# A fused linear attention and two gated feed-forward layers on one core: the attention of the first four half-batches as one chain ahead of everything, with multiplications of a zero tile on TensorE

## The chip, the cores and the metric

The kernel runs on one core of one Trainium2 chip. A core has five engines with instruction queues of their own: TensorE (PE in the profile; its weight loads are shown apart as PEld), VectorE (DVE), ScalarE (ACT), GpSimd (POOL) and SyncE (SP). Each engine takes its instructions strictly in the order in which the program lists them, and waits on semaphores for what other engines or transfers must deliver first. Transfers between the chip's main memory and the on-chip memory are issued from the queues of SP, ACT and POOL and moved by 16 DMA engines. The metric is the device time of one execution in microseconds (us), lower is better; the profile adds one recorded execution.

## The reference

Eight batches with eight heads of 576 positions and 64 channels go through linear attention with a norm; the result, 4608 tokens of 512 channels, goes through two feed-forward layers, all in float32.

```python
kv  = einsum('bhsd,bhse->bhde', k, v)            # 64 x 64 for each head
out = einsum('bhsd,bhde->bhse', q, kv)
rms = sqrt(mean(out * out, axis=-1) + 1e-6)
x   = (out / rms * g_norm)                       # -> 4608 tokens x 512
h   = x @ w_in;  x = (h * cos(h)) @ w_out        # 512 -> 2048 -> 512
a, b = x @ w1, x @ w2                            # 512 -> 1024
out = ((a * b) @ w3) @ w_out2                    # 1024 -> 1024 -> 512
```

## The kernel before, in words

**Numbers.** TensorE multiplies tiles of a type that it takes in one pass and that holds fewer bits than float32. So each float32 operand is split into a high part (a rounding copy, on ACT) and a low part (source minus high part, on DVE or POOL), and a product is three multiplications: high by high, high by low, low by high (`split`, `three`). The kv products of the attention and the sums of squares take float32 tiles as they are.

**Units.** A unit is half a batch, 288 positions; units 0 and 1 are batch 0, units 2 and 3 batch 1, and so on to 15. Heads are taken in pairs (p = 0 to 3), two heads side by side on 128 partitions. For a pair of a batch `emit_kv` makes the two 64 x 64 products of k and v, `evac_kv` splits them into the tile `kv_sb[p]`; for a unit and a pair the queries are split (tile `qhl`), multiplied by kv (`out`), squared (`sq`, ACT) and copied with the norm's weight (`o`, ACT). Sums of squares come from a product with a small selection matrix `sel`. The inverse root is made by three rounds of Newton on DVE (`newton`, 11 small dependent instructions), and `o` is multiplied by it.

**Two ways for the inverse root.** `first_units` handles units 0 and 1: sums land in one PSUM tile `ms_first`, Newton runs on 96 partitions, and TensorE spreads the result over the partitions of `o` by multiplying it with an identity (`spread`). The other units go through `unit_stage`, stage by stage: sums (`ms`), out to main memory (`msd`), back in another shape (`rsx`), Newton, out again (`rsd`) and back as a broadcast (`bc`), four transfers in a row, before `emit_x` multiplies `o`.

**The first feed-forward layer.** Tokens are taken in 9 tiles of 512. A tile's tokens x are split by `split_x` into the tile `x_hl` (one buffer, 4 blocks c of 128 channels). A step n is one block m of 128 of the 2048 hidden channels: `emit_h` (12 multiplications of 128 x 512, into one of two PSUM buffers), the cosine gate on ACT and DVE (`g_first`, `g_rest`; the last DVE instructions of a step are u times h and the low part of g) and, two steps later, `emit_w` (12 more). The order of steps is tile 0 with m = 0 to 7, tile 1 with all 16, tile 0 with 8 to 15, then tiles 2 to 8. Tile 1 needs units 1, 2 and 3.

**Weights.** They arrive as 64-bit numbers and are turned into float32 on chip: a chunk of 128 x 512 takes one ACT instruction (`Abs`) and four on DVE (lines 143 to 150, names `i_f` and `u_f`), then `put` splits it into `w_in` or `w_out` (one ACT copy, one DVE subtraction). 32 chunks belong to the first layer. Eight are converted between `first_units` and the loop over steps, the rest by a rule in the loop.

**The order.** The program is written as above and a list scheduler orders each engine's instructions; an instruction that is written later can stand earlier if its inputs are expected earlier. Units 2 and 3 are written behind the first steps by a table, `quick`, which puts their stages behind steps 0 to 6; their loads go through POOL's queue (`queue(u)`) behind a small GpSimd instruction (`gate`). After the first layer the second one follows, with its weights combined on chip; the change doesn't touch it.

Of the kernel before, what the change touches and what calls it, by code (L numbers as in the profile page):

```python
# [7 lines left out]
F32 = mybir.dt.float32  # L8
# [26 lines left out]
def kernel(  # L35
# [240 lines left out]
    def evac_kv(b, p):  # L276

        ps = kv_ps.pop((b, p))
        for h in range(2):
            d = slice(D * h, D * (h + 1))  # L280
            split(kv_sb[p][d, :, d], ps[d, 0:D], nc.vector)

    def queue(u):

        return nc.gpsimd if 2 <= u < 4 else nc.sync

    def small(u):
        return None if u < 4 else nc.gpsimd
# [62 lines left out]
    def newton(x, y, t):  # L351
# [4 lines left out]
        for _ in range(3):  # L356
            nc.vector.tensor_tensor(t, x, y, ALU.mult)
            nc.vector.scalar_tensor_tensor(t, t, 0.5, y, ALU.mult, ALU.mult)
            nc.vector.scalar_tensor_tensor(y, t, 1.5, y, ALU.subtract, ALU.mult)
# [24 lines left out]
    def emit_x(u, p):  # L384
        o = o_sb[u][:, p, :]
        engine = nc.vector if u < 2 else even(HALF)
# [6 lines left out]
    def first_units(spread):  # L393

        for p in range(NPAIR):
            emit_kv(0, p)
            evac_kv(0, p)
            for u in range(2):
                if p == 0:
                    o_sb[u] = ap.tile([P, NPAIR, HALF], F32, tag="osb", bufs=3, name=f"o_{u}")  # L400
                hl = ap.tile([P, 2, HALF], F32R, tag="hl", bufs=2, name=f"qhl_{u}_{p}")
                split(hl, q_raw.pop((u, p)), nc.vector)
                ps = ps_acc.tile([P, 512], F32, tag=f"acc{(2 * p + u) % 4}", name=f"out_{u}_{p}")
                o, w = ps[:, 0:HALF], kv_sb[p]
# [3 lines left out]
                sq = ap.tile([P, HALF], F32, tag="tmp", bufs=5, name=f"sq_{u}_{p}")  # L408
                nc.scalar.activation(sq, o, AF.Square)
                nc.scalar.activation(o_sb[u][:, p, :], o, AF.Identity, scale=gneg)  # L410
                if p == NPAIR - 2 and u == 1:

                    gate = ap.tile([P, 1], F32, name="gate")
                    marks.append(
                        nc.gpsimd.tensor_tensor(gate, sq[:, 0:1], sq[:, 0:1], ALU.subtract)
                    )

                if p == 0 and u == 0:
                    mst = ps_h.tile([P, 512], F32, tag="h", name="ms_first")
                for k in range(NT3):  # L420
                    at = ((u * NT3 + k) * NPAIR + p) * 2
                    nc.tensor.matmul(
                        mst[0:T3, at:at + 2], sq[:, T3 * k:T3 * k + T3], sel[:, 0:2],
                        start=p == 0 and u == 0 and k == 0, stop=True, skip_group_check=True,
                    )
        n = 4 * NPAIR * NT3
        x, y, t = (row(f"rs_first_{i}")[0:T3, 0:n] for i in range(3))
        nc.vector.tensor_scalar(x, mst[0:T3, 0:n], EPS, HUGE, ALU.add, ALU.min)
        newton(x, y, t)
        for u in range(2):  # L430
            for p in range(NPAIR):
                ps = ps_acc.tile([P, 512], F32, tag=f"acc{p}", name=f"spread_{u}_{p}")
                for k in range(NT3):
                    at = ((u * NT3 + k) * NPAIR + p) * 2
                    for h in range(2):
                        nc.tensor.matmul(
                            ps[D * h:D * h + D, T3 * k:T3 * k + T3],
                            y[:, at + h:at + h + 1].to_broadcast([T3, D]), spread[0:T3],
# [715 lines left out]
```

## Time and profile before

| | us |
|---|---|
| median of 3 runs | 1528.47 (1526.98 to 1534.14) |
| the profiled execution, its own time | 1531.2 |
| its span, first to last instruction | 1529.4 |
| TensorE busy | 1490.5 (97% of the span) |
| VectorE busy | 929.7 (61%) |
| ScalarE busy | 697.0 (46%) |
| GpSimd busy | 370.4 (24%) |

The profiled execution's own time is 1.8 us over its span and 2.7 us over the median. Busy time is the sum of an engine's instructions; a matmul's end is modelled, so a busy TensorE isn't TensorE at its peak rate. Its clock has two levels here, 1.2 and 2.4 GHz; the column PEclk of the windows is the granted share of the higher.

### The profile page before, as it was taken

What the parts mean: (1) busy time and instruction counts of PE and PEld (TensorE: products, weight loads), DVE (VectorE), ACT (ScalarE), POOL (GpSimd) and SP (SyncE); (2) the same over time, 40 slices, a digit from 0 to 9 for tenths busy, and PEclk for the clock granted to TensorE, in tenths of its full rate; (3) what the DMA queues carried; (4) which work ended last, traced back from release to release, by engine and by line L of the source; (5) the groups of instructions that cost most, each with busy time, mean ns of one, the idle gap of its engine ahead of it and who ended that gap; (6) DMA issues with size and microseconds to landing.
All of it is one profiled execution on the core that took longest, in us unless ns stands there. A gap on an engine that the chain in (4) does not pass through costs nothing.

```text
span 1529.4 us, 20532 instructions
## 1 busy us (share of the span) xinstructions
PE 1490.5 (97%) x7616; PEld 1272.5 (83%) x7616; DVE 929.7 (61%) x1714; ACT 697.0 (46%) x1405; POOL 370.4 (24%) x301
## 2 busy tenths in 40 slices
PE   6799999999999999999999998999999999999998
PEld 6577888888887787888888887999999988999997
DVE  3899844576576576666766546755545546545543
ACT  4667654444454454444534335433433334333331
POOL 1111010110010121101102006455444237344330
PEclk9799999999999999999999999999999999999999
DMA  8655120433323424244222005121102313233312
GB/s 292 220 153 167 43 72 5 153 106 114 116 93 102 140 91 146 90 126 123 84 83 79 34 20 215 42 76 67 69 38 83 111 57 113 73 103 124 124 63 76
DMA packets 81956, 156.26 MB, mean 102 GB/s; under 512 B 11600, under 2 KB 37376, under 8 KB 81856
## 3 DMA queue, kind: packets, MB, share of 16 engines
q1 hardware_dynamic: 80240, 150.18, 30.5%
q0 software_dynamic: 1616, 4.78, 1.1%
q8 instruction: 59, 0.97, 0.3%
q14 instruction: 41, 0.34, 0.1%
HBM read 113.77 MB, written 41.15 MB: 101 GB/s over the span
## 4 chain that ended last, share of the span: by engine, by line
PE 86%; DVE 3%; DMA 3%; issue 1%; POOL 1%; ACT 1%; SPq 0%; DVEq 0%; ACTq 0%; POOLq 0%
PE X L767 13%; PE h L533 8%; PE x L535 8%; PE h L534 8%; PE h L535 8%; PE x L533 8%; PE x L534 8%; PE V L767 6%; PE o L534 4%; PE o L533 4%; PE o L535 4%; PE Y L767 3%; PE kv L273 1%; DMA bc<-rsd 1%; PE ms L333 1%
## 5 line engine op out<-in xcount | busy, mean ns | idle before, releaser
L767 PE MATMUL X<-xc,w 128*128 128x384 f32 x1152 | 224.8, 336 | 4.5 <-DVE wchl L115 2.3
L535 PE MATMUL x<-g,w_out 128*128 128x512 f32 x576 | 225.3, 391 | 0.0
L534 PE MATMUL x<-g,w_out 128*128 128x512 f32 x576 | 225.0, 391 | 0.0
L533 PE MATMUL h<-x,w_in 128*128 128x512 f32 x544 | 216.7, 399 | 3.4 <-DVE u L559 2.0
L534 PE MATMUL h<-x,w_in 128*128 128x512 f32 x544 | 214.4, 394 | 1.8 <-DVE x L115 1.8
L533 PE MATMUL x<-g,w_out 128*128 128x512 f32 x576 | 212.6, 391 | 1.5 <-ACT g L113 1.1
L535 PE MATMUL h<-x,w_in 128*128 128x512 f32 x544 | 213.9, 393 | 0.0
L767 PEld LDWEIGHTS X<-xc,w 128*128 128x128 f32 x1152 | 202.9, 188 | 12.1 <-ACT s L775 3.2
L115 POOL TENSOR_TENSOR xc<-x2r,xc 128x768 fp32r<-128x768 f32 x70 | 134.4, 1929 | 229.1 <-ACT xc L113 229.1
L547 ACT ACTIVATE u<-h 128x512 f32<-128x512 f32 x144 | 86.0, 598 | 151.3 <-PE h L535 147.9
L558 ACT ACTIVATE u<-u 128x512 f32<-128x512 f32 x144 | 91.0, 632 | 121.8 <-DVE u L554 107.4
L115 DVE TENSOR_TENSOR g<-u,g 128x512 fp32r<-128x512 f32 x144 | 105.2, 731 | 64.0 <-ACT g L113 63.8
L113 ACT ACTIVATE g<-u 128x512 fp32r<-128x512 f32 x144 | 91.0, 632 | 108.5 <-DVE u L559 85.4
L115 POOL TENSOR_TENSOR qhl<-q,qhl 128x288 fp32r<-128x288 f32 x48 | 42.7, 892 | 395.5 <-ACT qhl L113 316.1
L775 ACT ACTIVATE s<-X 128x384 f32<-128x384 f32 x144 | 66.6, 488 | 152.4 <-PE X L767 152.2
L533 PEld LDWEIGHTS h<-x,w_in 128*128 128x128 f32 x544 | 103.4, 190 | 29.7 <-DVE u L559 5.8
L533 PEld LDWEIGHTS x<-g,w_out 128*128 128x128 f32 x576 | 107.7, 188 | 24.3 <-ACT g L113 1.2
L534 PEld LDWEIGHTS x<-g,w_out 128*128 128x128 f32 x576 | 108.6, 189 | 22.9 <-issue 0.5
L535 PEld LDWEIGHTS x<-g,w_out 128*128 128x128 f32 x576 | 108.4, 188 | 22.8
L559 DVE TENSOR_TENSOR u<-u,h 128x512 f32<-128x512 f32 x144 | 98.5, 684 | 47.2 <-ACT u L558 46.8
L553 DVE TENSOR_SCALAR r<-u 128x512 f32<-128x512 f32 x112 | 49.8, 445 | 123.8 <-ACT u L547 123.7
L534 PEld LDWEIGHTS h<-x,w_in 128*128 128x128 f32 x544 | 103.4, 190 | 23.5 <-DVE x L115 2.5
(183 smaller groups left out, 2653.8 us busy)
## 6 DMA issues: line engine op xcount, KB each, us to landing
x2r<-x_all SPq DMA_DIRECT2D x44, 384.0 KB
kvraw<-in_kv_main_dram SPq DMA_DIRECT2D x28, 512.0 KB
x_all<-x2s SPq DMA_DIRECT2D x36, 256.0 KB
part<-o SPq DMA_DIRECT2D x36, 256.0 KB
part<-part SPq DMA_DIRECT2D x36, 256.0 KB
out_dram<-part SPq DMA_DIRECT2D x36, 256.0 KB
i_w<-in_w1pair_dram SPq DMA_DIRECT2D x16, 512.0 KB
u_w<-in_w1pair_dram SPq DMA_DIRECT2D x16, 512.0 KB
```

The lines of the kernel that those rows point to most:

```text
L113: hi = nc.scalar.activation(dst[:, 0], src, AF.Copy)
L115: lo = lo_engine.tensor_tensor(dst[:, 1], src, f32(dst[:, 0]), ALU.subtract)
L273: nc.tensor.matmul(ps[d, 0:D], k[:, d], v[:, d], start=i == 0, stop=i == NC)
L533: nc.tensor.matmul(ps, w[0], x[0], start=first, stop=False)
L534: nc.tensor.matmul(ps, w[0], x[1], start=False, stop=False)
L535: nc.tensor.matmul(ps, w[1], x[0], start=False, stop=last)
L547: nc.scalar.activation(u, h_ps[n], AF.Identity, bias=0.25, scale=INV_2PI)
L553: nc.vector.tensor_scalar(r, u, ROUND, ROUND, ALU.add, ALU.subtract)
L558: nc.scalar.activation(u, u, AF.Sin, scale=-TWO_PI_DOWN)
L559: nc.vector.tensor_tensor(u, u, h_ps.pop(n), ALU.mult)
L767: nc.tensor.matmul(ps, w[:, self.i, a, k], x[:, b, k], start=first and k == 0 and n == 0, stop=last and k == 1 and n == 2, skip_group_chec ...
L775: copied.append(nc.scalar.activation(s, ps, AF.Copy).ins)
```

## The change

What it does:

- All four units of batches 0 and 1 go through `first_units`, as one chain of eight steps (b, p), written in the order in which the engines are to take it; inside `manual_schedule` the scheduler leaves DVE, ACT and PE in that order. A step is: products with the queries (`outs`), squares, then kv, queries and kv's split of the next pair, then sums of squares of this one, four multiplications of a zero tile (`idle_work`: 256 columns, result never read), the weighted copies, and, behind pairs 1 and 3 to 7, a weight chunk converted (`convert(1)`) and an earlier one split (`put(1)`).
- 28 multiplications of the zero tile stand ahead of the first kv product.
- The queries' high part is a copy on DVE instead of ACT; kv's split does both high parts, then both low parts.
- Newton runs once, on 96 x 96 numbers for four units instead of 96 x 48 for two; units 2 and 3 get their inverse root through `spread` too. The four transfers in a row, the table `quick` and `gate` are gone for them.
- Loads: queries come for both units of a batch at once, pairs 0 and 1 on ACT's queue; batch 0 and the first weight chunks on SP's; batch 1 and the norm's weight on POOL's. A buffer of batch 0 is used again by batch 1.
- Behind the chain six more chunks are converted instead of eight; `issue_after` orders them and the spreads of units 2 and 3 behind Newton and behind the spreads of units 0 and 1. In the loop, stages of units up to step 31 are ordered behind step n - 2, and their loads behind a weight load.

The diff, cut to its core:

```diff
     def evac_kv(b, p):
         ps = kv_ps.pop((b, p))
-        for h in range(2):
-            d = slice(D * h, D * (h + 1))
-            split(kv_sb[p][d, :, d], ps[d, 0:D], nc.vector)
+        halves = [slice(D * h, D * (h + 1)) for h in range(2)]
+        for d in halves:
+            nc.scalar.activation(kv_sb[p][d, 0, d], ps[d, 0:D], AF.Copy)
+        for d in halves:
+            nc.vector.tensor_tensor(
+                kv_sb[p][d, 1, d], ps[d, 0:D], f32(kv_sb[p][d, 0, d]), ALU.subtract
+            )
     def queue(u):
-        return nc.gpsimd if 2 <= u < 4 else nc.sync
+        return nc.sync
...
+    def load_first():
...
+        qs(0, 0, nc.scalar)
+        qs(0, 1, nc.scalar)
+        kv(0, 0, nc.sync)
+        rest(0, nc.sync)
+        kv(0, 1, nc.sync)
+        prefetch(1)
+        for p in (2, 3):
+            kv(0, p, nc.sync)
+            qs(0, p, nc.sync)
+        rest(1, nc.gpsimd)
         for p in range(NPAIR):
-            emit_kv(0, p)
-            evac_kv(0, p)
-            for u in range(2):
...
+            kv(1, p, nc.gpsimd)
+            qs(1, p, nc.gpsimd)
+        prefetch(8)
...
+        def queries(b, p):
+            for u in range(NHALF):
+                hl = hls[:, (2 * p + u) % 4]
+                q = q_raw.pop((NHALF * b + u, p))
+                nc.vector.tensor_copy(hl[:, 0], q)
+                nc.vector.tensor_tensor(hl[:, 1], q, f32(hl[:, 0]), ALU.subtract)
...
+        for i, (b, p) in enumerate(order):
+            outs(b, p)
+            square(b, p)
+            if i + 1 < len(order):
+                emit_kv(*order[i + 1])
+                queries(*order[i + 1])
+                evac_kv(*order[i + 1])
+            sums(b, p)
+            for _ in range(4):
+                idle_work()
+            keep(b, p)
+            if i in CONVERT:
+                convert(1)
+                if i > CONVERT[0]:
+                    put(1)
+        put(1)
+        nc.vector.tensor_scalar(x, mst[0:T3, 0:NR], EPS, HUGE, ALU.add, ALU.min)
+        last = newton(x, y, t)
...
+    CONVERT = (1, 3, 4, 5, 6, 7)
...
-        first_units(spread)
-        for c in range(KD):
-            split_x(0, c)
-        for _ in range(4):
+        with tc.manual_schedule(
+            engines={
+                mybir.EngineType.DVE, mybir.EngineType.Activation, mybir.EngineType.PE
+            }
+        ):
+            nc.vector.tensor_scalar(gneg, gneg, -1.0, None, ALU.mult)
+            warm = ps_h.tile([P, 512], F32, tag="h", name="warm")
+
+            def idle_work():
+                nc.tensor.matmul(
+                    warm[:, 0:2 * P], kv_warm[:, 0],
+                    kv_warm, start=True, stop=True,
+                )
+
+            for _ in range(28):
+                idle_work()
...
+        for k in range(3):
             prefetch(state["conv"] + 8)
             convert(2)
             put(2)
+        for p in range(NPAIR):
+            rows_of(1, p)
...
-            for u, s in quick.get(n, ()):
-                one = [unit_stage(u, s)]
-                for i in range(4):
-                    run(one, i)
```

How it moves instructions, at two places. First TensorE at the start, around the products of pair 0 with the queries (`out_0_0` is unit 0, pair 0; `kv_0_1` batch 0, pair 1; `warm` the zero tile's result). Before, all four kv products of the batch stand ahead of these rows:

```order
L405 MATMUL out_0_0_159<-qhl_0_0_156,kv0_82 128x288
L406 MATMUL out_0_0_159<-qhl_0_0_156,kv0_82 128x288
L405 MATMUL out_1_0_174<-qhl_1_0_171,kv0_82 128x288
L406 MATMUL out_1_0_174<-qhl_1_0_171,kv0_82 128x288
L407 MATMUL out_0_0_159<-qhl_0_0_156,kv0_82 128x288
L407 MATMUL out_1_0_174<-qhl_1_0_171,kv0_82 128x288
L422 MATMUL ms_first_166<-sel_86,sq_0_0_163 96x2 x3
L405 MATMUL out_0_1_202<-qhl_0_1_199,kv1_83 128x288
```

Now the same engine from the last of the six products of pair 0 on:

```order
L470 MATMUL out_1_0_224<-qhl_first_199,kv0_82 128x288
L273 MATMUL kv_0_1_234<-kvraw_0_1_123 64x64 x8
L273 MATMUL kv_0_1_234<-kvrest_0_121 64x64 x2
L489 MATMUL ms_first_200<-sel_86,sq_0_0_229 96x2 x3
L489 MATMUL ms_first_200<-sel_86,sq_1_0_232 96x2 x3
L1010 MATMUL warm_170<-zeros_97 128x256 x4
L468 MATMUL out_0_1_265<-qhl_first_199,kv1_83 128x288
```

The kv product of the next pair, all sums and four zero products now stand between the products of one pair and of the next, eight times in place of four.

Second VectorE around Newton. Before, Newton (`rs_first`) is mixed with the conversion of the first chunks (`i0_f`, `i1_f`) and with units 2 and 3 (`qhl_2_0` is unit 2, pair 0):

```order
L147 SCALAR_TENSOR_TENSOR i0_f_420<-i0_w_404,i0_f_420 128x512
L144 TENSOR_SCALAR i1_f_423<-i1_f_423 128x512
L359 SCALAR_TENSOR_TENSOR rs_first_1_310<-rs_first_2_311,rs_first_1_310 96x48
L115 TENSOR_TENSOR kv0_82<-kv_1_0_552,kv0_82 64x64
L115 TENSOR_TENSOR qhl_2_1_593<-q_2_1_550,qhl_2_1_593 128x288
L150 SCALAR_TENSOR_TENSOR i0_f_420<-i0_w_404,i0_f_420 128x512
L147 SCALAR_TENSOR_TENSOR i1_f_423<-i1_w_406,i1_f_423 128x512
L357 TENSOR_TENSOR rs_first_2_311<-rs_first_0_309,rs_first_1_310 96x48
```

Now, from Newton's last instruction to the first multiplication of o by the inverse root (`o_0`):

```order
L363 SCALAR_TENSOR_TENSOR rs_first_108<-rs_first_108 96x96
L143 TENSOR_SCALAR i4_f_708<-i4_f_708 128x512
L143 TENSOR_SCALAR u2_f_711<-u2_f_711 128x512
L143 TENSOR_SCALAR i5_f_730<-i5_f_730 128x512
L143 TENSOR_SCALAR u3_f_733<-u3_f_733 128x512
L143 TENSOR_SCALAR i6_f_752<-i6_f_752 128x512
L144 TENSOR_SCALAR i4_f_708<-i4_f_708 128x512
L144 TENSOR_SCALAR u2_f_711<-u2_f_711 128x512
L144 TENSOR_SCALAR i5_f_730<-i5_f_730 128x512
L144 TENSOR_SCALAR u3_f_733<-u3_f_733 128x512
L533 TENSOR_TENSOR o_0_228<-o_0_228,spread_0_0_614 128x288
```

Newton now stands alone behind the whole chain, and five chunks (i4, u2, i5, u3, i6) are converted between it and the last piece of tile 0's split. Counted over the whole list, VectorE has up to that last piece 33 instructions of 128 x 512 with two inputs, 23 with one, 30 of 128 x 288 with two inputs and 4 of 128 x 224, 16 copies of 128 x 288, 16 of 64 x 64 and 11 of Newton.

## Rows read from the trace of the kernel before

**Rows 1.** The page: engines (part 1) and the chain that ended last (part 4).

```profile
PE 1490.5 (97%) x7616; PEld 1272.5 (83%) x7616; DVE 929.7 (61%) x1714; ACT 697.0 (46%) x1405; POOL 370.4 (24%) x301
PE 86%; DVE 3%; DMA 3%; issue 1%; POOL 1%; ACT 1%; SPq 0%; DVEq 0%; ACTq 0%; POOLq 0%
```

**Rows 2.** Windows: stretch, length, busy us of PE, PEld, DVE, ACT, POOL; PEclk, DMA share, GB/s.

```profile
10.00:20.00 10.00, 9.65 (x72) 8.73 (x68) 3.75 (x13) 6.17 (x19) 0.00 (x0) 1.00 0.92 276
...
0.00:58.80 58.80, 41.65 (x355) 34.57 (x356) 35.49 (x98) 31.73 (x80) 8.64 (x26) 0.91 0.83 283
...
58.80:71.30 12.50, 8.13 (x36) 4.95 (x35) 8.61 (x18) 9.01 (x22) 3.07 (x5) 0.91 0.55 178
71.30:112.00 40.70, 40.69 (x209) 31.61 (x209) 37.24 (x89) 26.79 (x55) 7.91 (x11) 0.94 0.50 145
112.00:120.50 8.50, 5.47 (x36) 4.01 (x33) 8.50 (x23) 7.05 (x20) 1.81 (x1) 0.80 0.65 178
120.50:160.00 39.50, 38.84 (x182) 29.96 (x181) 36.16 (x82) 28.87 (x60) 5.73 (x6) 1.00 0.45 140
```

**Rows 3.** Timeline of DVE: start, duration, line, operation, idle before and releaser.

```profile
11.20 0.15 DVE L893 TENSOR_SCALAR gneg<-gneg 128x1 f32<-128x1 f32 x1 [0.55 <-DMA gneg<-in_g_norm_dram]
...
28.07 0.20 DVE L358 SCALAR_TENSOR_TENSOR rs_first<-rs_first,rs_first 96x48 f32<-96x48 f32 x1
28.31 0.20 DVE L359 SCALAR_TENSOR_TENSOR rs_first<-rs_first,rs_first 96x48 f32<-96x48 f32 x1
...
57.46 0.42 DVE L144 TENSOR_SCALAR i_f<-i_f 128x512 int32<-128x512 int32 x1
57.80 0.68 DVE L147 SCALAR_TENSOR_TENSOR u_f<-u_w,u_f 128x512 int32<-128x512 int32 x1
58.40 0.38 DVE L115 TENSOR_TENSOR x<-o,x 128x224 fp32r<-128x224 f32 x1
...
59.30 0.45 DVE L115 TENSOR_TENSOR qhl<-q,qhl 128x288 fp32r<-128x288 f32 x1
59.67 0.68 DVE L150 SCALAR_TENSOR_TENSOR u_f<-u_w,u_f 128x512 int32<-128x512 int32 x1
...
67.07 0.42 DVE L143 TENSOR_SCALAR u_f<-u_f 128x512 f32<-128x512 f32 x1
67.53 0.43 DVE L144 TENSOR_SCALAR u_f<-u_f 128x512 int32<-128x512 int32 x1
```

**Rows 4.** Timeline of PE, three stretches.

```profile
9.52 1.12 PE L273 MATMUL kv<-kvraw 128*64 128x64 f32 x16
...
10.99 1.12 PE L273 MATMUL kv<-kvraw 128*64 128x64 f32 x16
...
13.09 0.44 PE L405 MATMUL out<-qhl,kv 128*128 128x288 f32 x1
13.33 0.44 PE L406 MATMUL out<-qhl,kv 128*128 128x288 f32 x1
...
71.31 0.80 PE L533 MATMUL h<-x,w_in 128*128 128x512 f32 x1 [1.30 <-DVE u L559]
...
126.83 0.29 PE L315 MATMUL out<-qhl,kv 128*128 128x288 f32 x1
126.96 0.29 PE L316 MATMUL out<-qhl,kv 128*128 128x288 f32 x1
```

**Rows 5.** Timeline of ACT: the squares of unit 0, pairs 0 and 3.

```profile
14.05 0.41 ACT L409 ACTIVATE sq<-out 128x288 f32<-128x288 f32 x1 [0.44 <-PE out L407]
...
24.80 0.41 ACT L409 ACTIVATE sq<-out 128x288 f32<-128x288 f32 x1 [1.41 <-PE out L407]
```

**Rows 6.** The chain that ended last, in order of time: start, us, what.

```profile
109.90 3.69 DMA bc<-rsd
```

**Rows 7.** Windows of 2 us later in the first layer, columns as in rows 2.

```profile
504.00:506.00 2.00, 1.49 (x24) 1.38 (x25) 0.58 (x2) 0.22 (x1) 1.77 (x2) 1.00 0.12 48
506.00:508.00 2.00, 2.00 (x7) 1.54 (x6) 0.23 (x1) 1.35 (x4) 0.69 (x1) 0.52 0.58 152
```

More of the change, by code (lines that the diff above doesn't have):

```diff
@@ L428, in first_units @@
[L428 to L438, printed above, removed]
-                            start=k == 0, stop=True, skip_group_check=True,
-                        )
-                o = o_sb[u][:, p, :]
-                nc.vector.tensor_tensor(o, o, ps[:, 0:HALF], ALU.mult)
+                o_ps[NHALF * b + u, p] = o
@@ new lines, in first_units @@
+        order = [(b, p) for b in range(2) for p in range(NPAIR)]
+        emit_kv(*order[0])
+        queries(*order[0])
+        evac_kv(*order[0])
+        for i, (b, p) in enumerate(order):
[13 more added lines that the diff above has]
+                    put(1)
@@ new lines, in rows_of @@
+        def rows_of(b, p):
+            for u in range(NHALF * b, NHALF * b + NHALF):
+                if b == 0:
+                    ps = ps_acc.tile(
+                        [P, 512], F32, tag=f"acc{(2 * p + u) % 4}", name=f"spread_{u}_{p}"
+                    )
+                else:
+                    ps = ps_a.tile([P, 512], F32, tag="pa", name=f"spread_{u}_{p}")
+                mm = scaled(u, p, ps)
+            return mm
+        for p in range(NPAIR + 1):
+            if p < NPAIR:
+                mm = rows_of(0, p)
+            if p > 0:
+                split_x(0, p - 1)
@@ L878 @@
         )
+        for h in range(2):
+            nc.gpsimd.dma_start(
+                out=gneg[D * h:D * h + D], in_=g_norm.rearrange("(d o) -> d o", o=1)
+            )
         def run(stages, i):
@@ L932 @@
             if n < NS:
-                stages = [unit_stage(u, n - w) for u, w in windows.items() if 0 <= n - w <= LAST]
+                with tc.issue_after(word_loads[min(n + 9, n_first - 6)].ins):
+                    stages = [
+                        unit_stage(u, n - w) for u, w in windows.items() if 0 <= n - w <= LAST
+                    ]
                 if more > 0:
@@ L938 @@
                 uu = g_first(n)
-            run(stages, 0)
-            run(stages, 1)
+            gate = ExitStack()
+            if n < 2 * NM:
+                for ins in since[:3 * (n - 1)][-3:]:
+                    gate.enter_context(tc.issue_after(ins))
+            with gate:
+                run(stages, 0)
+                run(stages, 1)
             if n >= 2 and not swap:
                 emit_w(n - 2)
-            run(stages, 2)
+            with ExitStack() as gate:
+                if n < 2 * NM:
+                    for ins in since[:3 * (n - 1)][-3:]:
+                        gate.enter_context(tc.issue_after(ins))
+                run(stages, 2)
             if n < NS:
@@ L954 @@
                         split_x(after, c)
-            run(stages, 3)
-            for u, s in quick.get(n, ()):
-                one = [unit_stage(u, s)]
-                for i in range(4):
-                    run(one, i)
+            with ExitStack() as gate:
+                if n < 2 * NM:
+                    for ins in since[:3 * (n - 1)][-3:]:
+                        gate.enter_context(tc.issue_after(ins))
+                run(stages, 3)
+            if n == 2:
+                behind.close()
             if n == NM + 4:
```

157 lines of the change are left out of this document (103 added, 54 removed), and 3 rows, old and new, of the table quick.

## The prediction

> **What bounds the kernel now.** I read the page first: TensorE is busy 97% of the span and makes 86% of the chain that ended last [rows 1]. So time can only come from stretches in which TensorE waits or runs at its lower clock. The windows show where these lie [rows 2]: in the first 71.3 us TensorE is busy for 41.65 + 8.13 us, and once more from 112 to 120.5, where it is busy 5.47 of 8.5 us. From 120.5 to 160 it lacks 0.66 us. Three moments of the timelines mark the beginning. **A**, 58.8 us: VectorE ends the last piece of tile 0's split (the row at 58.40 lasts 0.38) [rows 3]. **B**, 71.3 us: the third step's first multiplication, let go by VectorE's product u times h [rows 4]. From B on TensorE is busy 40.69 of 40.7 us until the stall at 112 [rows 2]. That stall follows the last transfer of the broadcast for tile 1, which lands at 109.90 + 3.69 = 113.6 [rows 6]; VectorE then has the split of tile 1 to do, in a stretch where it is busy all 8.50 us.
>
> What sets A? VectorE has been busy 35.49 of 58.8 us by then [rows 2], so it waited for 23.3. The change must be judged by VectorE's work up to A, its waits up to A, and the way from A to B; behind B the kernel is TensorE's.
>
> The clock: the granted share reads 1.00 from 10 to 20 us [rows 2], but products of 288 columns stand 0.24 us apart at 13 us and 0.13 apart at 127 us [rows 4], so the chain of before ran at 1.2 GHz, the lower level, and I go by the spacing.
>
> **The change, part by part.** *VectorE's work up to A.* Paces are starts that follow each other [rows 3]: 0.34 us for one input of 512 (57.46 to 57.80), 0.60 for two (57.80 to 58.40), 0.37 for two of 288 (59.30 to 59.67). With the counts given with the change: 33 x 0.60 = 19.8; 23 x 0.34 = 7.8; 34 x 0.37 = 12.6, the four of 224 taken as 288. The copy of 288 with one input isn't in the trace: between 0.19 (0.34 by columns) and 0.37; I take 0.25 since it has one input, 16 x 0.25 = 4.0. The 64 x 64 ones lie between 0 and 0.37, at 0.2 make 3.2. Newton on 96 numbers in a row lies between 0.24 (28.07 to 28.31, 48 numbers) and twice that; fixed cost weighs more at this size, 11 x 0.3 = 3.3. Sum 50.7 us, against 35.5 before: the queries' high parts, units 2 and 3 and four more chunks have moved ahead of A.
>
> *Its waits up to A.* (1) VectorE's first real instruction waits for the norm's weight, which landed at 11.2 us behind four kv loads [rows 3]; it is now behind one small load on another queue. The first pair's loads, 1.3 MB, at 276 GB/s [rows 2] take 5 us and some 2 to start: 7 us. (2) Pairs 0 to 3 need 3.5 MB, and with batch 1's first loads and a weight chunk, which share the engines, about 5.5 MB: at 276 GB/s 20 us, so the split of pair 3's kv ends at about 23.4 us, when VectorE has done some 8 us of work. Issuing from three queues doesn't add to this rate. The Trainium skill says so too (DMA: Bandwidth & Descriptors, "Issuing engines are not separate DMA queues"); no run here separates the queues. (3) Pairs 4 to 7 are paced by an engine. VectorE: conversions now stand alone and depend on each other, which costs 0.46 in place of 0.34, 0.12 more for each (67.07 to 67.53 [rows 3]): a chunk 2 x 0.46 + 2 x 0.72 = 2.4, its split 0.6, queries 1.5, kv 0.4: 4.9 us a pair. TensorE at the lower clock: the pair of before took (24.80 - 14.05) / 3 = 3.58 [rows 5], a kv product 10.99 - 9.52 = 1.47, four zero products of 256 columns 4 x 0.213 = 0.85: 5.9 us a pair. At the higher clock it is near half of that and hidden under VectorE. (4) Behind the last pair: two chunks and three splits, 6.6, and Newton, 3.3.
>
> Newton's end: with the clock up, 23.4 + 3.0 (pair 4 has no chunk) + 3 x 4.9 + 9.9 = 51.0. With the clock down, the first products at 10.3, the eighth pair at 10.3 + 7 x 5.9 = 51.6, + 9.9 = 61.5.
>
> *From Newton to A and B.* 15 x 0.60 + 11 x 0.34 + 18 x 0.37 = 19.4 us, mostly chunk conversions that stand ahead of x. Then 6 us to B: twelve more VectorE instructions stand between the last split and the product that lets step 2 go (6 x 0.60 + 0.34 + 5 x 0.37 = 5.8). Before, this way took 12.5 us, as ACT and VectorE had units 2 and 3 to serve [rows 2]; half of it is saved. B comes at 76.4 with the clock up, 86.9 with it down; before, 71.3. Both ways TensorE has been mostly idle ahead of B, so step 2 starts at the lower clock as before.
>
> *Behind B.* Tile 1's units are ready long before step 8, so the broadcast is gone from the path. The stall was worth 3.03 us of idle time and 0.20 x 8.5 = 1.7 of clock [rows 2]. One buffer holds x, so tile 1's split still waits for step 7; the products of two steps cover it but for perhaps 1 us. I take 4 us back. Loads, stages and order of later tiles differ little: nothing.
>
> *The zero products ahead* take at most 28 x 0.213 = 6.0 us from about 1 us on: they end as the first data lands, and are hidden under it. If the data came at 4.5 us, they would cost 2.
>
> *Sum:* 76.4 - 71.3 - 4 = +1.1 us with the clock up throughout, +11.6 with it down throughout. I take a chain that starts at the higher clock and loses it for part of the pairs, B at 79.5: +4 us. The profiled execution lies 2.7 us above the median; on the median, 1528.5 + 4 = **1532 us**, 0.3% more. A measurement of this kernel can't tell less than 0.5%, 7.6 us, from no change, so I forecast: no change that can be measured.
>
> **The rivals.** *The clock stays down in the chain (slower).* Place: pairs 1 to 7. Price: 5.9 us a pair on TensorE in place of 4.9 on VectorE, B at 86.9, +11.6, so 1540. It decides as soon as TensorE needs over 4.9 us a pair. For it: the kernel of before kept TensorE busy for 9.65 of 10 us between 10 and 20 us with such products and sums of two columns, and it stayed at 1.2 GHz; and after one gap in the stretch 504 to 506, beside a kv product and three with queries, the granted clock was 0.52 [rows 7]. Against it: 28 dense products ahead and four between pairs, which that chain lacked. The Trainium skill speaks against the change here (TensorE: Matmul & The Clock Gate, "A second HAM failure mode: psum-queue depth-cycling"): micro-idles between groups of matmuls make the clock fall and rise again and again. The windows at 504 agree with it, and it would give this rival's 1540.
>
> *Loads come early enough that VectorE never waits after the first data (faster).* Then A comes at 7 + 50.7 + 3 (dependent instructions) = 60.7, B at 66.7, and 71.3 - 66.7 + 4 = 8.6 us are won: 1520. For it: VectorE had 23.3 us of waits to lose and its work is placed into them. Against it: 276 GB/s in the stretch where the loads were the same in kind [rows 2], and VectorE's fixed order, in which pair 3's queries stand ahead of the next conversion.
>
> *The stall at the tile's change stays.* Its 4 us aren't won: 1536 with the rest as forecast. Against it: the broadcast that it followed is gone.
>
> **How the numbers follow.** Forecast 0.45, its own range 1527 to 1537. Clock down 0.25 (1540). No waits 0.17 (1520). Stall stays, or other late waits, 0.13. Slower by over 0.5% (beyond 1536): the clock's 0.25 and most of the last, 0.33. Faster (under 1521): 0.17 and a little for prices that I set too high, 0.20. Within: 0.47. The range takes in the bounds on both sides, 1519 to 1541.
>
> **What would show it.** VectorE's busy time up to the last piece of tile 0's split near 51 us; that moment between 70 and 80 us; B 6 us behind it; conversions 2.4 us each in the chain; kv split of pair 3 at 23 us; no transfer `bc` ahead of step 8 and TensorE idle under 1 us there. The spacing of the products in pairs 4 to 7 tells the clock. I'd be wrong if pairs 0 to 3 come in under 20 us, if VectorE's copies and splits overlap better than their order lets me think, or if stalls behind 160 us, which I leave as they are, change.

## The result, and the profile after

The changed kernel's median is 1538.41 us (8 runs, 1536.36 to 1542.0); the kernel before, run beside it, has 1530.74. The ratio is 1.0051, 95% interval 1.0037 to 1.0066: 7.7 us slower, just over the 7.6 that I called no change, with an interval that reaches to both sides of that bound. The profiled execution took 1542.0, the slowest of the eight and 3.6 us above their median; its span is 1540.2, 10.8 us above the span before. What follows reads this execution.

Its page gives the span and each engine's busy time, and the slices of TensorE's granted clock:

```profile
span 1540.2 us, 20866 instructions
PE 1506.9 (98%) x7804; PEld 1291.6 (84%) x7804; DVE 936.5 (61%) x1709; ACT 693.2 (45%) x1387; POOL 362.0 (24%) x286
PEclk7599999999999999999999999999999999999999
```

TensorE is now idle for 1540.2 - 1506.9 = 33.3 us where it was 38.9, so the change did take idle time away, 5.6 us. But the groups of lines show 13.8 us of zero products:

```profile
L1010 PE MATMUL warm<-zeros 128*128 128x256 f32 x60 | 13.8, 390 | 1.2 <-DVE gneg L976 1.2
```

What is left, 1506.9 - 13.8 = 1493.1, is TensorE's own work, at whatever clock it got: 2.6 more than before's 1490.5. So 13.8 + 2.6 - 5.6 = 10.8. I split every kernel below in these three: idle, zero products, own work. Own work has the same 7744 products in all the changed kernels, so its differences among them come mostly from the clock (ends of products are modelled, so a microsecond more or less says little). The kernel before has 7616: there units 2 and 3 get their inverse root by transfers and not by TensorE.

The windows by stage, to set beside [rows 2], with the same columns: A is now 80.7, B 87.2.

```profile
0.00:58.80 58.80, 47.10 (x364) 42.37 (x364) 32.32 (x82) 27.29 (x67) 8.67 (x24) 0.69 0.66 240
58.80:80.70 21.90, 17.50 (x151) 14.81 (x152) 21.55 (x56) 7.15 (x15) 0.00 (x0) 0.58 0.49 153
80.70:87.20 6.50, 4.81 (x67) 3.32 (x65) 6.04 (x13) 3.95 (x7) 0.00 (x0) 1.00 0.77 251
112.00:128.00 16.00, 15.88 (x71) 12.83 (x70) 15.78 (x38) 11.36 (x28) 0.00 (x0) 1.00 0.04 16
```

The last row is the tile's change: no stall is left there (15.88 of 16 us), and no instruction on `bc` stands ahead of it.

VectorE's timeline at the beginning and at A and B (start, duration, then the instruction, and in brackets what ended the idle time ahead of it):

```profile
10.77 0.15 DVE L1006 TENSOR_SCALAR gneg<-gneg 128x1 f32<-128x1 f32 x1 [9.61 <-DMA gneg<-in_g_norm_dram]
10.84 0.30 DVE L458 CAST qhl_first<-q 128x288 fp32r<-128x288 f32 x1
...
28.30 0.46 DVE L283 TENSOR_TENSOR kv<-kv,kv 64x64 fp32r<-64x64 f32 x2 [0.60 <-ACT kv L281]
...
61.39 0.26 DVE L363 SCALAR_TENSOR_TENSOR rs_first<-rs_first 96x96 f32<-96x96 f32 x1
...
79.94 0.75 DVE L115 TENSOR_TENSOR x<-o,x 128x288 fp32r<-128x288 f32 x2
...
86.51 0.68 DVE L667 TENSOR_TENSOR u<-u,h 128x512 f32<-128x512 f32 x1
```

The multiplication of the norm's weight still heads VectorE's queue and waits until 10.77; all splits of queries stand behind it. TensorE's timeline shows what that does:

```profile
6.72 0.69 PE L273 MATMUL kv<-kvraw 128*64 128x64 f32 x16
11.29 0.37 PE L468 MATMUL out<-qhl_first,kv 128*128 128x288 f32 x1 [3.62 <-DVE qhl_first L458]
12.79 0.61 PE L469 MATMUL out<-qhl_first,kv 128*128 128x288 f32 x1 [1.13 <-DVE kv L283]
13.19 0.45 PE L470 MATMUL out<-qhl_first,kv 128*128 128x288 f32 x1
13.43 0.45 PE L468 MATMUL out<-qhl_first,kv 128*128 128x288 f32 x1
18.69 0.44 PE L468 MATMUL out<-qhl_first,kv 128*128 128x288 f32 x1
30.64 0.44 PE L468 MATMUL out<-qhl_first,kv 128*128 128x288 f32 x1
35.03 0.29 PE L468 MATMUL out<-qhl_first,kv 128*128 128x288 f32 x1
35.16 0.30 PE L469 MATMUL out<-qhl_first,kv 128*128 128x288 f32 x1
40.93 0.61 PE L469 MATMUL out<-qhl_first,kv 128*128 128x288 f32 x1 [1.75 <-DVE kv L283]
87.24 0.50 PE L639 MATMUL h<-x,w_in 128*128 128x512 f32 x1 [0.85 <-DVE u L667]
```

The first kv product, right behind the zero products, runs at the higher clock (16 in 0.69 us, where before they took 1.12 [rows 4]). Then TensorE waits 3.62 us and 1.13 more, and from 13.19 on the products with the queries (below: the heads' products) stand 0.24 us apart: 1.2 GHz, for pairs 0 to 3, six microseconds a pair from pair 1 on. Pair 4 has 0.13; in pair 5 a wait of 1.75 us follows the first product, and the others and pair 6 have 0.24 again; pair 7 has 0.13. Stages of the clock:

```profile
12.80:32.00 19.20, 19.20 (x131) 17.59 (x131) 9.24 (x26) 7.33 (x20) 4.37 (x7) 0.50 1.03 400
32.00:40.00 8.00, 6.94 (x81) 5.90 (x79) 4.23 (x11) 5.88 (x16) 0.00 (x0) 0.93 0.32 98
56.00:77.00 21.00, 13.80 (x128) 12.05 (x129) 20.49 (x50) 9.30 (x19) 0.00 (x0) 0.50 0.41 126
```

In the last of them TensorE does the spread and most of step 0 at 0.50. Step 32's product u times h starts at 273.78, before at 263.67: 10.1 of the 10.8 us are there by then.

### The profile page after: what moved, and what is told of

The parts are those of the page before. It is cut to its first block, busy times and chain, and to the rows that moved or that the text cites. A ratio compares the mean times of both kernels' runs of the same rounds, so it can differ in the third digit from the quotient of the medians.

```text
span 1540.2 us, 20866 instructions
## 1 busy us (share of the span) xinstructions
PE 1506.9 (98%) x7804; PEld 1291.6 (84%) x7804; DVE 936.5 (61%) x1709; ACT 693.2 (45%) x1387; POOL 362.0 (24%) x286
## 4 chain that ended last, share of the span: by engine, by line
PE 88%; DVE 5%; DMA 3%; issue 1%; POOL 1%; ACT 1%; SPq 0%; DVEq 0%; ACTq 0%; POOLq 0%
PE X L875 13%; PE h L639 8%; PE x L639 8%; PE x L641 8%; PE x L640 8%; PE h L641 8%; PE h L640 8%; PE V L875 6%; PE o L640 4%; PE o L639 4%; PE o L641 4%; PE Y L875 3%; PE kv L273 2%; DMA kvraw<-in_kv_main_dram 1%; PE ms_first L489 1%
## 5 line engine op out<-in xcount | busy, mean ns | idle before, releaser
L639 PEld LDWEIGHTS x<-g,w_out 128*128 128x128 f32 x576 | 107.8, 188 | 22.6 <-issue 0.5
```

The costliest lines, as they stand in the source:

```text
L639: nc.tensor.matmul(ps, w[0], x[0], start=first, stop=False)
```

## The experiments

**Theory.** The clock made the difference: the chain lost the clock in the wait for the norm's weight, and TensorE's time, not VectorE's work, decides. **Rivals:** the zero products between pairs cost what was lost; or VectorE's way from Newton's end to A does, where five chunks stand ahead of x.

All ran beside the kernel before, whose median was 1530.7 to 1531.0. Newton's end, B and the three parts are those of the one profiled execution; where a chain loses the clock differs from one execution to the next, so medians decide. An execution can lie far from its kernel's median: besides the changed kernel's (3.6 us above) the one of `late_12_conv` lies 4.3 us above and that of `gneg_late_16` 3.7 us below.

| kernel | median (runs) | ratio, 95% | Newton's end | B | span | idle | zero | own work |
|---|---|---|---|---|---|---|---|---|
| before | | | | 71.3 | 1529.4 | 38.9 | 0 | 1490.5 |
| changed | 1538.4 (8) | 1.0037 to 1.0066 | 61.7 | 87.2 | 1540.2 | 33.3 | 13.8 | 1493.1 |
| no_zeros | 1538.2 (6) | 1.0029 to 1.0064 | 59.2 | 84.8 | 1536.7 | 36.7 | 0 | 1500.0 |
| only_ahead | 1537.4 (6) | 1.0029 to 1.0062 | 59.8 | 85.4 | 1535.9 | 31.7 | 4.9 | 1499.3 |
| gneg_late | 1533.2 (12) | 1.0002 to 1.0024 | 56.1 | 81.7 | 1530.6 | 26.9 | 14.0 | 1489.7 |
| gneg_late_none | 1534.5 (11) | 1.0019 to 1.0038 | 56.0 | 81.9 | 1532.7 | 34.0 | 0 | 1498.7 |
| gneg_late_16 | 1538.6 (6) | 1.0029 to 1.0063 | 52.5 | 78.3 | 1533.1 | 28.3 | 23.1 | 1481.7 |
| between_16_60 | 1544.1 (4) | 1.0081 to 1.0107 | 60.6 | 85.6 | 1544.0 | 31.8 | 29.5 | 1482.7 |
| conv_later | 1539.1 (6) | 1.0039 to 1.0070 | 59.9 | 83.5 | 1535.8 | 33.0 | 12.7 | 1490.1 |
| late_12_conv | 1532.4 (12) | 1.0004 to 1.0030 | 54.3 | 78.9 | 1534.9 | 30.7 | 19.6 | 1484.6 |
| late_12_conv_60 | 1528.5 (12) | 0.9966 to 0.9987 | 55.2 | 76.5 | 1528.3 | 22.6 | 26.9 | 1478.8 |
| late_12_60 | 1526.9 (12) | 0.9971 to 0.9994 | 51.9 | 75.2 | 1523.3 | 21.1 | 25.1 | 1477.1 |
| late_0_40 | 1529.9 (11) | 0.9987 to 1.0008 | 54.8 | 78.1 | 1526.8 | 24.9 | 7.5 | 1494.4 |
| late_12_conv_60_8 | 1526.5 (9) | 0.9967 to 0.9985 | 52.5 | 75.3 | 1525.1 | 20.8 | 26.6 | 1477.7 |

### Are the zero products worth their time?

`no_zeros` leaves out all of them, `only_ahead` those between the pairs (the second piece alone):

```diff
-            for _ in range(28):
-                idle_work()
...
-            for _ in range(4):
-                idle_work()
```

> No zero products at all: neither the 28 ahead of the chain nor the 4 behind each pair. Theory (the clock is low through most of the chain anyway, since it fell in the wait of 3.6 us for VectorE at 7.7 us, and so the 4 products only lengthen TensorE's row): pairs 0 to 3 start 5.1 us apart where it was 5.97, the Newton row ends 2 to 5 us earlier than 61.65, the first matmul of step 2 comes at 82 to 85 where it was 87.2, and the median is 2 to 4 us below the changed kernel's. Rival (the 4 products are what lets the clock rise at 33 us and so hold pairs 4 and 5 to 3.8 us): the granted clock stays at 0.50 up to the Newton row, step 2 begins at 87 or later, and the median is the changed kernel's or up to 3 us above it.

> The 28 zero products stay, the 4 behind each pair are gone. Theory (the high clock that the 28 bought is lost in the wait behind them, before the first product of a head): as the kernel without any zero product, within 1 us, since nothing but the 20 small products of pair 0's keys and values runs at the high clock. Rival (what the 28 did lives on into the chain once the 4 don't lengthen it): some pairs start under 5 us apart at a granted clock near 1.00, and step 2 begins over 3 us earlier than without any zero product.

Without any, the median is the changed kernel's (0.2 us below it): the theory's 2 to 4 us did not come, and the rival's median did, though B came earlier, at 84.8. Rows of TensorE's timeline (the first kv product, and the heads' products of pairs 2 and 3) and one window of this kernel:

```profile
4.60 1.12 PE L273 MATMUL kv<-kvraw 128*64 128x64 f32 x16 [4.60 <-DMA kvraw<-in_kv_main_dram]
22.85 0.59 PE L468 MATMUL out<-qhl_first,kv 128*128 128x288 f32 x1
23.48 0.44 PE L470 MATMUL out<-qhl_first,kv 128*128 128x288 f32 x1
23.72 0.44 PE L468 MATMUL out<-qhl_first,kv 128*128 128x288 f32 x1
27.97 0.59 PE L468 MATMUL out<-qhl_first,kv 128*128 128x288 f32 x1
12.80:50.00 37.20, 37.17 (x270) 33.39 (x271) 24.76 (x64) 19.99 (x52) 4.42 (x7) 1.00 0.69 263
```

Pairs come 5.12 us apart (22.85 to 27.97) with 0.24 between products, so the whole chain ran at 1.2 GHz, with TensorE busy 37.17 of 37.20 us. (The window's granted clock reads 1.00, as it did in the chain of before: the spacing tells, not this column.) The zero products of the change take 13.8 us of TensorE's time; 36.7 - 33.3 = 3.4 of these are idle time here, and 1500.0 - 1493.1 = 6.9 come back from the stretches at the higher clock. In these two executions the changed kernel is left 3.5 us behind, by the medians 0.2: no gain either way. With only the 28 it is the same within 0.9 us, as the theory said: the 28 alone bought nothing that lived through the wait. They also hold back the first kv product, which starts at 4.60 us here and behind them at 6.72; the wait for the weight covers that.

### The wait for the norm's weight

`gneg_late` moves one instruction; `gneg_late_none` does so without any zero products; `gneg_late_16` has 16 between pairs in place of 4.

```diff
-            nc.vector.tensor_scalar(gneg, gneg, -1.0, None, ALU.mult)
             warm = ps_h.tile([P, 512], F32, tag="h", name="warm")
...
         evac_kv(*order[0])
+        nc.vector.tensor_scalar(gneg, gneg, -1.0, None, ALU.mult)
```

> One instruction moved: VectorE multiplies gneg by -1 behind the first pair's splits instead of ahead of them, so that the queries of pair 0 no longer stand behind gneg's DMA. Theory (that wait starts the chain 3.8 us late and costs the clock that the 28 zero products bought): the first product of a head starts at 8 to 9.5 us where it was 12.79, behind less than 2 us of idle TensorE, the granted clock stays at 1.00 through pairs 0 and 1 at least, the pairs come at VectorE's pace of 4.9 us, the Newton row ends at 50 to 55 us where it was 61.65, step 2 begins at 76 to 81, and the median is 5 to 9 us below the changed kernel's. Rival (TensorE's share of work in the chain is too small to hold the clock, whoever starts it): the chain starts 4 us earlier, the clock falls in the first pairs all the same, the pairs come 5.9 us apart, step 2 begins at 83, and the median is 2 to 4 us lower.

> gneg's multiplication moved as before, and no zero products at all. Theory (with the wait gone the zero products do little: VectorE, not TensorE's clock, is next): the chain starts at 8.5 to 9.5 at the low clock (0.24 us between products), the pairs come 5.1 us apart, the Newton row ends at 55 to 56.5 and step 2 begins at 80 to 82.5, so the median is within 1.5 us of the kernel with gneg moved and its zero products (1533.2). Rival (the zero products are what made that kernel's gain, by the two pairs at the high clock that they bought): step 2 begins at 84 or later, and the median is 1536 or more.

> As the kernel with gneg's multiplication moved, with 16 zero products behind each pair instead of 4. Theory (enough of them hold the clock up, and at the high clock they fit beside VectorE's row): 1.8 us of heads, 0.7 of keys and values and 1.7 of zero products are 4.2 us a pair, under VectorE's 4.9; the granted clock is 1.00 from 9 us to the Newton row, that row ends at 50 to 52, step 2 begins at 75 to 78, and the median is 8 to 11 us below the changed kernel's. Rival (the clock falls in some wait all the same): a pair then takes 3.6 + 1.5 + 3.4 = 8.5 us, each pair at the low clock ends 3.6 us later than at VectorE's pace, and with four of them or more step 2 begins at 90 or later.

The move alone brings 5.2 us back, as the theory said (5 to 9), and B from 87.2 to 81.7. Its VectorE and TensorE:

```profile
5.64 0.31 DVE L458 CAST qhl_first<-q 128x288 fp32r<-128x288 f32 x1 [4.49 <-DMA q<-in_qt_dram]
10.85 0.15 DVE L504 TENSOR_SCALAR gneg<-gneg 128x1 f32<-128x1 f32 x1 [1.31 <-DMA gneg<-in_g_norm_dram]
9.08 0.37 PE L468 MATMUL out<-qhl_first,kv 128*128 128x288 f32 x1 [0.66 <-issue]
12.93 0.29 PE L468 MATMUL out<-qhl_first,kv 128*128 128x288 f32 x1
18.21 0.61 PE L469 MATMUL out<-qhl_first,kv 128*128 128x288 f32 x1 [1.37 <-DVE kv L283]
```

The queries have landed by 5.64; in the changed kernel their splits wait five microseconds more for a weight that nothing needs yet. The chain starts with 0.13 us between products, and loses the clock in the third pair, in a wait of 1.37 us. The next pairs come 5.97 us apart, as the rival had it, so Newton's end (56.1) and B come later than the theory's 50 to 55 and 76 to 81. Without zero products the late multiplication is still worth 1538.2 - 1534.5 = 3.7 us: the start itself, since the first of the heads' products there starts at 7.69 us where without the move it is 11.33. The zero products add 1.4, within the theory's 1.5; behind the 28 the first of the heads' products starts 1.4 us later (9.08), and no run separates the 28 from the 4.

With 16 between pairs the theory was right on the clock up to the last pair, and wrong on the time. The pairs of this kernel come 4.81 us apart; the last two rows are from tile 1's steps:

```profile
18.69 0.29 PE L468 MATMUL out<-qhl_first,kv 128*128 128x288 f32 x1
18.96 0.30 PE L470 MATMUL out<-qhl_first,kv 128*128 128x288 f32 x1
23.50 0.29 PE L468 MATMUL out<-qhl_first,kv 128*128 128x288 f32 x1
137.85 0.50 PE L640 MATMUL h<-x,w_in 128*128 128x512 f32 x1 [2.69 <-DVE u L668]
140.25 0.63 PE L642 MATMUL h<-x,w_in 128*128 128x512 f32 x1
```

Over the span own work falls by 8.0 us, and the zero products take 9.1 more: no gain. Up to B there is one, 78.3 against 81.7; it is lost behind B, for step 32's product u times h starts at 268.08, in `gneg_late` at 266.53. In between TensorE waits 2.69 us for the gate (VectorE's product u times h), where `gneg_late` waits 0.8. From 1.5 us behind the wait on its products stand 0.43 us apart where they stood 0.23, until 143 us; `gneg_late` is granted 1.00 there. Wait and clock make some 3.4 of these 5 us: 1.9 of wait, and 1.5 by which ten products from 139.39 to 143.22 take longer than at 0.23 each. Why the wait is longer here is open. The median is even 5.4 above `gneg_late`; the rest of that isn't in this profile, which is of the fastest of the six executions.

`between_16_60` is the changed kernel, weight first as there, with 16 between the pairs and 60 behind the last:

```diff
-            for _ in range(4):
+            for _ in range(16 if i + 1 < len(order) else 60):
```

> The changed kernel with 16 zero products behind each pair and 60 behind the last, and gneg's multiplication left where the change has it. Theory (dense work brings the clock back by itself, also after the wait at the beginning): the chain starts at 12 to 13 us at the low clock, the clock is up before the fourth pair and stays up to the Newton row, step 2 begins at 81 to 84, and the median is 1531 to 1535: late start and two pairs of 8.5 us, but the rest at the high clock. Rival (after the wait at the beginning the chain keeps the low clock as it did with 4 zero products): five pairs or more take 8.5 us, the Newton row ends at 70 or later, and the median is 1542 or more.

```profile
13.98 0.44 PE L468 MATMUL out<-qhl_first,kv 128*128 128x288 f32 x1
21.79 0.44 PE L468 MATMUL out<-qhl_first,kv 128*128 128x288 f32 x1
22.36 0.30 PE L468 MATMUL out<-qhl_first,kv 128*128 128x288 f32 x1
26.77 0.29 PE L468 MATMUL out<-qhl_first,kv 128*128 128x288 f32 x1
```

The clock comes back in the second pair and stays, as the theory said; the time is the rival's. It is 17.3 us slower than `late_12_60` below, which has the weight's multiplication behind and 12 instead of 16: a late start costs its wait, the first pair at the lower clock with all its zero products (the rows at 13.98 and 21.79), and here 2.9 us in one wait for the gate at 144 us as well, behind which the clock falls (0.72 from 144 to 150).

### VectorE's chunks on the way to A

`conv_later` converts two chunks less ahead of step 0:

```diff
-        for k in range(3):
+        for k in range(2):
             prefetch(state["conv"] + 8)
             convert(2)
             put(2)
```

> The changed kernel with one thing altered: two instead of three pairs of chunks are converted behind the Newton row, so that 10 chunks and not 12 are converted ahead of step 0; the steps convert the other two, at step 2. Theory (from the Newton row on, VectorE's row sets the first matmul of step 2, and these two chunks of 2.5 us each stand in it): the last split of tile 0 ends 3 to 4 us earlier than 80.7, step 2 begins at 82 to 83 where it was 87.2, and the median is 3 to 5 us below the changed kernel's. Rival (those 5 us of VectorE's work are owed anyway: behind step 2 VectorE is 95 % busy, so they come back as a wait of TensorE in steps 2 to 6 or at the tile change): step 2 begins as early, but TensorE then waits 3 us or more between 90 and 160, and the median is within 1 us of the changed kernel's.

The rival held: B is 3.8 us earlier (1.8 of that is there at Newton's end, ahead of which the edit changes nothing), the median 0.7 later. At step 32's product u times h 0.6 us are left of the lead (273.20 against 273.78). TensorE's waits from 84 to 160 us (us in total, times, longest) and the longest of them in its timeline show where it went:

```profile
PE h L639 <- DVE u L667: 4.5, 3, 2.7
145.09 0.50 PE L639 MATMUL h<-x,w_in 128*128 128x512 f32 x1 [2.69 <-DVE u L667]
```

The same product in the changed kernel:

```profile
144.93 0.50 PE L639 MATMUL h<-x,w_in 128*128 128x512 f32 x1 [0.94 <-DVE u L667]
```

TensorE waits 4.5 us for the gate where the changed kernel's waits on that line were 1.8. The wait at B itself is in both sums (1.55 and 0.85); behind B it is 3.0 against 0.9, 2.69 in one place for 0.94, which is 2 of the 3.2 us that the lead loses by step 32. VectorE owes the two chunks either way. So the end doesn't hang on where these two chunks stand, and B by itself is a poor measure.

### Filling TensorE's idle time instead

From the last pair to Newton's end TensorE has nothing to do. These kernels put zero products there, with the weight's multiplication behind as above: `late_12_conv` has 12 everywhere and 10 chunks ahead, `late_12_conv_60` has 60 behind the last pair, `late_12_60` the same with all 12 chunks, `late_12_conv_60_8` 8 more behind the first pair's heads, and `late_0_40` none, also not the 28, but 40 behind the last pair.

```diff
-            for _ in range(4):
+            for _ in range(0 if i + 1 < len(order) else 40):
```

> The three parts together: gneg's multiplication moved, 12 zero products behind each pair, 10 chunks instead of 12 converted ahead of step 0. Theory (the clock holds with 12 as it did with 16, VectorE's row is next and two chunks shorter): 0.13 us between the products of a head from 8.5 us to the last pair, the Newton row ends at 50 to 52.5, step 2 begins at 72.5 to 75 (78.3 with 16 zero products and all chunks, less 4 to 5), and with the 1450 to 1455 us that lie behind it in the kernels so far the median is 1525 to 1530, below the kernel before by 1 to 6. Rival (VectorE's work moved behind step 2 comes back as a wait, most likely at the change of tile at 112 to 120 us): step 2 begins as early, the rest takes 1458 us or more, and the median is 1531 to 1535.

> As the kernel with the three parts together, with 60 zero products behind the last pair instead of 12, which fill TensorE's idle time up to the end of the Newton row. Theory (VectorE's row sets step 2, so TensorE's clock ahead of it is worth little): the products of step 0 come 0.21 to 0.23 us apart where they were 0.43, but step 2 begins within 1.5 us of the kernel with 12, and the median is within 1.5 us of it. Rival (at the low clock the products of step 0 end late enough to hold back the gate's row for step 2): step 2 begins 2 to 4 us earlier and the median is 2 to 4 us lower.

> gneg's multiplication moved, 12 zero products behind each pair and 60 behind the last, and all 12 chunks converted ahead of step 0 as in the changed kernel. Theory (what counts is TensorE's time, its idle stretches and its stretches at the low clock, and not when VectorE does two chunks): step 2 begins 2 to 5 us later than the 76.5 of the kernel with 10 chunks, but its median, 1528.5, is met within 1.5 us. Rival (once TensorE's clock is up, VectorE's row is what sets step 2, and its 5 us come through to the end): the median is 1531 to 1534.

> gneg's multiplication moved; no zero products ahead of the chain or between the pairs, but 40 behind the last pair, where TensorE was idle in the kernel without any (from 50 to 56 us). Theory (zero products pay where TensorE would be idle and nowhere else): the chain is that of the kernel with gneg moved and no zero products (5.1 us a pair, Newton row to 55 or 56), the granted clock is 1.00 in the stretch of the spread and of step 0's products, where it was 0.50 from 64 to 70, and the median is 2 to 4 us below that kernel's 1534.5. Rival (the chain's own clock is where the gain of the 60 lay): the median is 1533.5 or more.

> The best so far (gneg moved, 12 and 60 zero products, 10 chunks) with 8 more zero products behind the first pair's heads, over the 1 us for which TensorE waited at 9.3 us for pair 1's keys and values, and in which the clock fell for 7 us. Theory (the chain's time at the low clock is TensorE's loss): 0.13 us between products from 8 us to the last pair, the Newton row ends 1.5 to 3 us earlier than 54.95, and the median is 1 to 3 us below that kernel's 1528.5. Rival (VectorE's row and its waits for ACT pace the pairs whenever the clock is up for most of them): the clock holds, but the Newton row ends within 1 us of 54.95, and the median is within 1 us.

`late_0_40` is the telling one: 4.6 us below `gneg_late_none`, more than the theory's 2 to 4, with the same chain at 1.2 GHz, and no difference from the kernel before (0.9987 to 1.0008). First step 0 without the 40 (`gneg_late_none`), then the 40 and step 0 with them:

```profile
68.77 0.63 PE L639 MATMUL h<-x,w_in 128*128 128x512 f32 x1
69.19 0.63 PE L640 MATMUL h<-x,w_in 128*128 128x512 f32 x1
```

```profile
47.81 7.45 PE L1010 MATMUL warm<-zeros 128*128 128x256 f32 x40
63.65 0.40 PE L642 MATMUL h<-x,w_in 128*128 128x512 f32 x1
63.89 0.39 PE L640 MATMUL h<-x,w_in 128*128 128x512 f32 x1
```

0.42 us between the first products of step 0 became 0.24 (from 70.4 us on it was 0.23 without the 40 too), and the first 60 products of the spread ahead of them took 3.06 us, without the 40 4.53. Own work fell by 4.3 us, idle time by 9.1, 7.5 of it filled. From Newton's end to B it takes 23.3 us in place of 25.9; another 1.2 us are there at Newton's end already, as TensorE waits 0.8 us less for pair 1's kv data in this execution. `late_12_conv` missed its theory (1525 to 1530) and fell to the rival's time, 1532.4, by another way than the rival's: its clock fell at the beginning, granted 0.63 from 12 to 20 us, behind a stretch in which TensorE waited 1.03 us for pair 1's kv data. The 60 then brought 3.9 us, as the rival of that run had it, not the theory. Chunks ahead or behind made no difference that shows: `late_12_60` is, if anything, 1.7 better, just beyond its theory's 1.5, but its B came 1.3 us earlier and not 2 to 5 later, since its chain kept the higher clock from 8 to 43 us where that of `late_12_conv_60` was granted 0.59 from 12 to 20. Covering the wait for pair 1's data with 8 more brought 2.1, as the theory of that run said, though the two ratios' intervals overlap; its Newton row ended 2.7 us earlier. And beside `late_0_40` the 28 ahead, 12 between pairs and 20 more behind (`late_12_60`) brought 3.1, against that run's theory that zero products pay in TensorE's idle time and nowhere else; the two intervals just touch (0.9971 to 0.9994, 0.9987 to 1.0008).

`late_12_60` and `late_12_conv_60_8` are the best, 0.2% below the kernel before: the changed kernel with two and four small edits, none of them to its arithmetic. Every run here keeps the rest of the change, the queries' high parts on VectorE, the order of the loads and the one Newton for four units; what each of these costs or brings isn't shown. Of the theory the first half is borne out: start and clock of TensorE's work are what these edits changed, and they bring the time back. The second half goes too far, since in three kernels waits for VectorE's gate behind B took back what was won ahead of it.

## Why the prediction was right, and what in it was wrong

The time lies in the range, which was wide enough to take in both rivals, but 6.4 us above the forecast, and beyond the 1536 up to which I had called it no change. Of these 6.4 us 2.3 are the kernel before, whose median was 1528.5 in three runs and 1530.7 beside this one; the change itself costs 7.7, half way between the 4 that I forecast and the 11.6 of my first rival, the clock that stays down. That rival describes what happened. **The step that failed** is the last of the sum: "I take a chain that starts at the higher clock and loses it for part of the pairs, B at 79.5". But for the first kv product and the first product with the queries, the chain started at the lower clock, and had the higher one for the heads of two pairs, 4 and 7. In the profiled execution, the slowest of eight, B came at 87.2, where my sum for the lower clock had 86.9. That is in part luck: the heads started at 11.3 us and were in full pace from 12.8, not at 10.3, and the pairs at the higher clock gave that back. Step by step:

- *Step (1), first data at 7 us.* The first kv data were there at 4.6 us (`no_zeros`) and the queries at 5.6 (`gneg_late`); the norm's weight, behind "one small load on another queue", landed at 10.8. I had named that instruction as the first of VectorE's queue, and did not ask what stands behind it. This also took the use from the 28 zero products, which bought nothing (`only_ahead`). I called them hidden under the first data; they outlasted these by 2 us, the case that I had priced at 2, and were hidden only under the wait for the weight. Moving the one instruction brings 5.2 us.
- *Step (2), 276 GB/s.* The transfers moved 400 GB/s from 12.8 to 32 us, so 276 wasn't a bound. Pair 3's kv split ended at 28.8, not 23.4, yet by TensorE's pace and not by the loads: in `gneg_late_16` the kv product of pair 3 starts at 19.58.
- *Step (3).* TensorE's 5.9 us a pair at the lower clock: 5.97 (18.69 to 30.64, two pairs). VectorE's 4.9: where the clock is up, pairs with a chunk came 4.9 to 5.0 apart (`late_12_60`: heads at 31.52, 36.45 and 41.47).
- *Work up to A.* 50.7 predicted, 32.32 + 21.55 = 53.9 measured; the copies took 0.30 us, not 0.25, which makes 0.8, and the 24 conversions in the chain were busy for 0.43 and 0.69 us, not 0.34 and 0.60, which makes 2.2; under (3) I had reckoned with that, but not here.
- *Newton's end, A, B.* 61.65 against 61.5 for the lower clock; then 19.0 us to A against 19.4, and 6.5 to B against 6. Step 2 began at the higher clock (its first product takes 0.50 us, before 0.80 [rows 4]), not at the lower as I said, and lost it behind B (0.64 from 87.2 to 92).
- *Behind B.* B moved by 15.9, the span by 10.8: 5.1 back, against 4. The stall at the tile's change is gone.
- *The rivals.* No waits: VectorE waited 26.8 of the first 80.7 us. Stall stays: it didn't. The clock: it fell behind the waits of 3.62 and 1.13 us and again behind that of 1.75, but it also stayed down in 37.2 us in which the profile shows 0.03 us of idle time (`no_zeros`); what keeps it down there is open. The Trainium skill names micro-idles between groups of matmuls as what makes the clock fall and rise (TensorE: Matmul & The Clock Gate, "A second HAM failure mode: psum-queue depth-cycling"). The falls behind the waits agree with it, the 37.2 us don't.

A fault of the method is that I counted to B. `conv_later` and `between_16_60` have an earlier B than the changed kernel, and `gneg_late_16` than `gneg_late`, and by their medians they are not faster; what was saved ahead of B came back behind it, as waits for VectorE's gate in all three.

## What to carry to other kernels

Where one engine is busy 97% of the time, count its own time: idle, useless work, and useful work at the clock it gets; an earlier milestone on the way is no gain if the work behind it is only postponed. Products that only keep the clock up paid most surely where the engine would be idle ahead of heavy work (4.6 us for 40 of them here). Inside the chain they went either way, from 5.4 us lost (16 a pair against 4) to 3.1 won (12 a pair, with 28 ahead and 20 more behind, beside the 40 alone), so they have to be measured. In an order fixed by hand, ask of each first instruction on a queue what waits behind it: a multiplication of 128 numbers, whose result is first read five microseconds later, cost 5.2 us here.

## What the runs showed of the hardware

- TensorE stayed at 1.2 GHz for 37.2 us in which the profile, with its modelled ends of products, has it busy for 37.17 (`no_zeros`): a busy TensorE in the profile is not one that gets the higher clock.
- In the same stretch the granted clock reads 1.00, so the column can be wrong at the beginning of a trace; the spacing of equal products (0.24 or 0.13 us for 288 columns) tells the two levels apart.
- One wait in dense work was followed by the lower clock: behind 2.69 us TensorE was granted 0.57 from 139.4 to 143.2 us (`gneg_late_16`), behind 0.8 us at the same product 1.00 (`gneg_late`).
- The load of the norm's weight, 0.2 KB, took a median of 6.6 us from issue to landing while other loads were in flight; loads of 256 and 288 KB from the same queue took 6.7 and 6.8.
